# Loads ahead of masks, batch 1's attention at other slots, and a down-projection by tile in a windowed-attention and mixer kernel

## The chip, the core and the metric

The kernel runs on one NeuronCore of a Trainium2 chip. The metric is the device time of one execution in microseconds (us). PE is the TensorE matmul engine, PEld its weight load, DVE the VectorE, ACT the ScalarE, POOL the GpSimd engine, SP the queue of SyncE. SBUF is the on-chip memory, PSUM the memory that PE writes and DVE and ACT read. L247 is line 247 of the kernel.

## What is computed

Eight batches of 576 tokens, eight heads of 64. Each token attends to itself and the 63 tokens before it. The result x (576 x 512 for each batch) is mixed over tokens by two low-rank matrices U (576 x 32) and V (32 x 576) and passes a two-layer network with a skip.

```python
scores = scale * np.matmul(q, k.transpose(0, 1, 3, 2))
mask = (rel >= 0) & (rel < 64)
attn = softmax(np.where(mask, scores, -1e9))
x = heads_side_by_side(np.matmul(attn, v))
u = x + (x.transpose(0, 2, 1) @ U @ V).transpose(0, 2, 1)
out = u + np.maximum(u @ w_ch1, 0.0) @ w_ch2
```

Inputs and output are float32; the loads on POOL's queue turn them into bf16.

## The kernel before

The order of each engine's work is the order of the code; nothing reorders it. An instruction waits for semaphores of what it reads or overwrites.

**Attention of one batch** (`attention(b)`) is a set of pieces. T: for each of four head pairs j, PE transposes K (`TK`) and Q (`TQ`) to have the head dimension on the partitions; ACT copies K's transpose to `kt[j]`, DVE copies Q's to `qt[j]`. The transposes write PSUM tiles of the pool `ps_tp`, which has one buffer (batch 0 also uses `ps_mm`, with three). S: scores of a head pair in blocks of 64 queries and 128 keys (`SC`, PSUM pool `ps_big`, two buffers), the exponential on ACT, and a product with the 0/1 mask `maskA` on DVE; `SC8` does the ninth block of all pairs. PV: for a token tile t, the products with V and a column of ones, then the reciprocal of the sums and x on DVE (`rcp`, `xs`). U: x times the matrix U into 32-row strips of one PSUM tile (`pshh`, in the text also the down-projection), copied to `hh` by ACT. V: `hh` times the matrix V (`psv`, the up-projection) plus x gives u (`un`). For batches 0 and 1 (`alone`) a second matmul with the identity adds x, and the result is copied; later batches add x on DVE. UT: transposes of u to `uTc`, the input of the network.

**K and Q** of batches below NGR = 4 are loaded "grouped": 96 partitions, each with six neighbouring tokens, so that a row of one head is 6 x 64 x 4 = 1,536 bytes in DRAM. Their transposes take twelve matmuls for a head pair. From batch 4 on a row is one token of one head (256 bytes), loaded in ten DMAs a batch into `kn` and `qn`, and a head pair takes five transposes (`tpn`). `vB` holds V moved by 64 tokens; most of it is copied from `vA` on POOL (`shift_v`).

**The network** works in nine chunks of 512 tokens (`mlp(c)`): 16 groups of 4 matmuls for the first layer (`psA`, with a ReLU on ACT or DVE), then 16 groups of 4 for the second (`psU`; after every fourth group DVE adds u into `osb`, and SP stores it). A chunk's 32 groups are its slots 0 to 31. After each slot stand the attention pieces that the tables PLACE, PLACE_1 (batch 1) and PLACE_2 (batch 2) name for it; slot 32 stands behind the last group. Chunk c carries the rest of batch c + 1's attention. Batch 0's stands ahead of all chunks.

**POOL's queue** issues the loads of K, Q, V and the weights, and also builds the identity and the masks and does the V copies, all in the code's order. Eight semaphores serve its DMAs in turn, so that a DMA waits for the one eight before it. At the start it issues two of batch 0's eight K/Q pieces, builds the identity, issues two, builds the mask, and issues the last four.

Of the kernel before, what the change touches and what calls it, by code (L numbers as in the profile page):

```python
# [17 lines left out]
def kernel(  # L18
# [24 lines left out]
    NGR = 4  # L43
# [120 lines left out]
    nc.gpsimd.affine_select(  # L164
        out=maskA[:, :, 0, :],
        in_=maskA[:, :, 0, :],
        compare_op=ALU.is_ge,
        fill=0.0,
        base=0,
        pattern=[[0, 2], [1, W]],  # L170
        channel_multiplier=-1,
    )
    nc.gpsimd.affine_select(
        out=maskA[:, :, 1:, :],
        in_=maskA[:, :, 1:, :],
        compare_op=ALU.is_ge,
        fill=0.0,
        base=-1,
        pattern=[[0, 2], [0, NB - 2], [-1, W]],
        channel_multiplier=1,  # L180
    )
    nc.gpsimd.affine_select(
        out=maskA[:, :, 1:, :],
        in_=maskA[:, :, 1:, :],
        compare_op=ALU.is_ge,
        fill=0.0,
        base=W,
        pattern=[[0, 2], [0, NB - 2], [1, W]],
        channel_multiplier=-1,
    )  # L190
    for _ in kq0:
        pass
    load_v(0)
# [32 lines left out]
    def attention(b, spare=False, alone=False):  # L226
# [10 lines left out]
        def tr(src, j):  # L237
            if grouped:
                if spare and turn[0] % 4 != 0:
                    tpb = ps_mm.tile([P, 2 * CH], BF16, name="tpm", tag="mm")  # L240
                    tp = tpb[:, 0:S].rearrange("d (c p) -> d c p", c=GR)
                else:
                    tp = ps_tp.tile([P, GR, GP], BF16, name="tpg", tag="tp")
                turn[0] += 1
                for c in range(GR):
                    for g in range(2):
                        nc.tensor.transpose(  # L247
                            tp[g * D : (g + 1) * D, c, :], src[:, 2 * j + g, c, :], ident[0:GP, 0:GP]
                        )
                return tp.rearrange("d c p -> d p c")  # L250
            tp = ps_tp.tile([P, NT, P], BF16, name="tpn", tag="tp")
            for t in range(NT):
                nc.tensor.transpose(  # L253
                    tp[:, t, :],
                    src[:, t, 2 * j : 2 * j + 2, :].rearrange("p h d -> p (h d)"),
                    ident[:],
                )
            return tp.rearrange("d t p -> d (t p)")[:, 0:S]
# [9 lines left out]
        def TQ(j):  # L268
            def f():
                nc.vector.tensor_copy(out=like(qt[j][:]), in_=tr(qb, j))  # L270
            return f
# [71 lines left out]
        def U():  # L343
            ps = ps_big.tile([P, 2, CH], FP32, name="pshh", tag="big")
            for t in (0, 1, 2, 3, 4):
                g = t % 4
                nc.tensor.matmul(  # L347
                    ps[g * R : (g + 1) * R, 0, :],
                    ub[odd][:, t, :],
                    x[:, t, :, :].rearrange("p h d -> p (h d)"),  # L350
                    start=(t < 4),
                    stop=(t == 4 or t in (1, 2, 3)),
                )
            hh["sb"] = wk_pool.tile([P, CH], BF16, name="hh", tag="hh")
            nc.scalar.copy(out=hh["sb"][:], in_=ps[:, 0, :])  # L355

        def VM(ts):
            def f():
                ps = ps_big.tile([P, 2, CH], FP32, name="psv", tag="big")
                for n, t in enumerate(ts):  # L360
# [6 lines left out]
                        stop=not alone,  # L367
                    )
                    if alone:
# [7 lines left out]
                for n, t in enumerate(ts):  # L377
# [5 lines left out]
                    if alone:  # L383
                        copy = nc.scalar.copy if n else nc.vector.tensor_copy
                        copy(out=u_tiles[g][lo:hi, :], in_=ps[lo:hi, n, :])
                        continue
# [28 lines left out]
        pcs["U"] = [U]  # L415
# [7 lines left out]
    def mlp(c):  # L423
# [65 lines left out]
    PLACE_2["S"] = [3, 5, 7, 9, 10]  # L489
# [4 lines left out]
    for j in range(HP):  # L494
        a["T"][2 * j]()
        a["T"][2 * j + 1]()
        if j > 0:
            a["S"][j - 1]()
        if j == 1:
            for i in range(2):  # L500
                nc.vector.tensor_copy(out=ub[i][:], in_=uf[i][:])
            nc.vector.tensor_copy(out=vrep[:, W : W + S], in_=vf[:])
    a["S"][HP - 1]()
    a["S"][HP]()
    for _ in load_kq(2, False):
        pass
    for f in a["PV"]:
        f()
    for part in ("U", "V", "UT"):
        for f in a[part]:  # L510
            f()
    load_v(2)


    for c in range(NCH):
# [10 lines left out]
        if b < B:  # L526
            shift_v(b, nc.gpsimd.tensor_copy)
            if 3 <= b + 1 < B:
                load_v(b + 1)
            if 4 <= b + 2 < B:  # L530
# [3 lines left out]
            if b <= 2:  # L534
                place(b, ("T",), where)
            place(b, ("S", "PV"), where)
# [3 lines left out]
            if b == 1:  # L540
                slots[NSLOT - 4].append(lambda: [None for _ in load_kq(3, False)])
# [34 lines left out]
```

## Time and profile before

| what | us |
|---|---|
| three runs, median (lowest, highest) | 368.05 (364.64, 369.66) |
| the profiled execution, its own time | 367.98 |
| its span | 366.2 |
| PE busy / DVE / ACT / POOL | 341.7 / 182.5 / 123.7 / 112.1 |

The profile is of one execution. Its span is the time from the first to the last instruction. A row of the timeline gives the start, the time and the engine of an instruction or of several alike in a row, what it writes and reads, and in brackets how long the engine was idle before it and what ended that. A matmul row's time includes its way through the array, so that neighbours overlap; the distance between two starts is what a matmul costs in a stream.

### The profile page before, as it was taken

The numbers are of one execution on the slowest core, as the hardware profiler recorded it, in microseconds if no ns is written. First come the engines' busy times: TensorE is split into PE (matmuls) and PEld (weight loads), VectorE is DVE, ScalarE is ACT, GpSimd is POOL, SyncE is SP. The second block draws the span as 40 slices with busy tenths as digits, with TensorE's granted clock in tenths as the row PEclk, the third lists the DMA queues.
The fourth block names the chain that finished last, engine by engine and source line by source line (L and its number), as shares of the span: only waits on it lengthen the run. The fifth ranks groups of instructions, "written<-read, shape, count | busy, mean of one in ns | idle before, by whom it ended". The sixth has DMA issues, their size and how long they took to land.

```text
span 366.2 us, 7144 instructions
## 1 busy us (share of the span) xinstructions
PE 341.7 (93%) x3082; PEld 168.1 (46%) x3082; DVE 182.5 (50%) x319; ACT 123.7 (34%) x188; POOL 112.1 (31%) x128
## 2 busy tenths in 40 slices
PE   2779997689999999999999999999999999999995
PEld 1534444334454445544554455445544444444442
DVE  4763425935665357535753575257535753322321
ACT  2604323136513362346233522462236213301300
POOL 8891172793079004570448034000000000000000
PEclk9999999989999999999999999999999999999999
DMA  8999999795099107990869047100120011011002
GB/s 123 147 210 207 189 184 183 114 142 38 3 87 167 57 2 46 109 157 2 54 89 169 0 32 94 57 2 2 42 74 0 2 60 57 0 42 74 0 35 82
DMA packets 91135, 28.69 MB, mean 78 GB/s; under 512 B 77152, under 2 KB 85344, under 8 KB 91104
## 3 DMA queue, kind: packets, MB, share of 16 engines
q0 software_dynamic: 84512, 18.36, 58.6%
q1 hardware_dynamic: 6592, 9.88, 7.9%
q8 instruction: 24, 0.39, 0.4%
q14 instruction: 7, 0.06, 0.1%
HBM read 37.14 MB, written 9.44 MB: 127 GB/s over the span
## 4 chain that ended last, share of the span: by engine, by line
PE 86%; DVE 6%; ACT 3%; POOL 2%; DMA 1%; issue 1%; ACTq 0%; POOLq 0%
PE psA L431 35%; PE psU L453 32%; PE xr L323 3%; PE tpn L253 3%; PE psv L362 3%; PE sc L277 3%; PE tpg L247 2%; PE tpu L404 2%; DMA kg<-in_k_dram 1%; DVE pts L293 1%; PE pshh L347 1%; DVE xs_97 L333 1%; ACT pts L292 1%; PE psv L370 1%; DVE xs_98 L333 1%
## 5 line engine op out<-in xcount | busy, mean ns | idle before, releaser
L431 PE MATMUL psA<-uTc,w1b 128*128 128x512 bf16 x576 | 132.9, 380 | 1.1 <-ACT uTc L409 1.1
L431 PEld LDWEIGHTS <-w1b 128*128 128x128 bf16 x576 | 53.0, 98 | 61.2 <-issue 1.1
L462 DVE TENSOR_TENSOR osb<-psU,un 128x512 f32<-128x512 f32 x36 | 24.8, 689 | 56.5 <-PE psU L453 56.4
L293 DVE TENSOR_TENSOR pts<-pts,maskA 128x1024 bf16<-128x1024 bf16 x32 | 24.4, 765 | 33.2 <-ACT pts L292 33.2
L292 ACT ACTIVATE pts<-sc 128x1024 bf16<-128x1024 f32 x32 | 32.6, 1022 | 13.1 <-PE sc L277 13.1
L124 POOL DMA_DIRECT2D vA_100<-in_v_dram x16 | 14.1, 885 | 44.4 <-PE xr L323 37.8
L409 ACT COPY uTc<-tpu 128x512 bf16<-128x512 bf16 x27 | 15.8, 585 | 28.2 <-PE tpu L404 28.2
L124 POOL DMA_DIRECT2D vA_99<-in_v_dram x16 | 14.1, 882 | 34.9 <-PE xr L323 29.0
L323 PEld LDWEIGHTS <-pts 128*64 128x64 bf16 x576 | 14.6, 115 | 20.3 <-issue 9.4
L362 PE MATMUL psv<-hh,vrep 128*128 128x512 bf16 x40 | 15.4, 434 | 1.3 <-ACT hh L355 1.3
L404 PEld LDWEIGHTS <-un 128*128 128x128 bf16 x144 | 11.1, 102 | 7.7 <-issue 0.6
L333 DVE TENSOR_TENSOR xs_98<-xr,rcp 128x512 bf16<-128x512 f32 (+1 forms) x20 | 13.8, 692 | 0.7
L333 DVE TENSOR_TENSOR xs_97<-xr,rcp 128x512 bf16<-128x512 f32 (+1 forms) x20 | 13.8, 690 | 0.7
L247 PE MATMUL tpg<-ident,kg 96*64 96x96 bf16 x168 | 6.7, 219 | 6.4 <-DMA kg<-in_k_dram 4.6
L332 DVE RECIPROCAL rcp<-xr 128x8 f32<-128x8 f32 (+1 forms) x40 | 8.1, 204 | 8.6 <-PE xr L323 8.6
L387 DVE TENSOR_TENSOR un<-psv,xs_98 128x512 bf16<-128x512 f32 (+1 forms) x15 | 9.8, 685 | 5.2 <-PE psv L362 5.2
L247 PEld LDWEIGHTS <-kg 96*64 96x64 bf16 x192 | 6.3, 122 | 13.3 <-DMA kg<-in_k_dram 7.3
L355 ACT CAST hh<-pshh 128x512 bf16<-128x512 f32 x8 | 4.7, 589 | 22.2 <-PE pshh L347 22.2
L404 PE MATMUL tpu<-ident,un 128*128 128x128 bf16 x120 | 11.8, 222 | 0.0
L323 PE MATMUL xr<-vA_100,pts 128*64 128x65 bf16 x160 | 9.1, 197 | 2.9 <-DVE xs_98 L333 1.5
L387 DVE TENSOR_TENSOR un<-psv,xs_97 128x512 bf16<-128x512 f32 (+1 forms) x15 | 9.5, 681 | 3.4 <-PE psv L362 3.4
L115 POOL DMA_DIRECT2D kn_104<-in_k_dram x10 | 8.8, 877 | 4.9 <-PE tpn L253 4.9
(575 smaller groups left out, 628.2 us busy)
## 6 DMA issues: line engine op xcount, KB each, us to landing
out_dram<-osb SPq DMA_DIRECT2D x36, 256.0 KB, 2.1
vA_99<-in_v_dram POOLq DMA_DIRECT2D x16, 128.0 KB, 5.7
w1b<-in_moe_w_ch_dram POOLq DMA_DIRECT2D x2, 1024.0 KB, 12.7
w2b<-in_moe_w_ch_dram POOLq DMA_DIRECT2D x2, 1024.0 KB, 15.7
vA_100<-in_v_dram POOLq DMA_DIRECT2D x16, 128.0 KB, 4.7
kg<-in_k_dram POOLq DMA_DIRECT2D x3, 576.0 KB, 13.6
qg<-in_q_dram POOLq DMA_DIRECT2D x3, 576.0 KB, 14.7
kn_103<-in_k_dram POOLq DMA_DIRECT2D x8, 128.0 KB, 4.3
```

The source lines that it names most:

```text
L124: nc.gpsimd.dma_start(out=va[:, t, :, 0:D], in_=v[b, :, t * P : (t + 1) * P, :].rearrange("h p d -> p h d"),)
L247: nc.tensor.transpose(tp[g * D : (g + 1) * D, c, :], src[:, 2 * j + g, c, :], ident[0:GP, 0:GP])
L292: nc.scalar.activation(out=dst, in_=sc[:], func=ACT.Exp, scale=scale)
L293: nc.vector.tensor_tensor(out=dst, in0=dst, in1=maskA.rearrange("p g n w -> p g (n w)"), op=ALU.mult)
L323: nc.tensor.matmul(xr[r0 : r0 + W, h // 4, (h % 4) * VW : (h % 4 + 1) * VW], pts[:, h // 2, h % 2, blk, :], rhs, start=True, stop=True,)
L333: nc.vector.tensor_tensor(out=x[lo:hi, t, :, :].rearrange("p (a h) d -> p a h d", a=2), in0=xv[:, :, :, 0:D], in1=rcp[lo:hi].to_broadcast( ...
L362: nc.tensor.matmul(ps[:, n, :], vrep[:, off : off + P], hh["sb"][:], start=True, stop=not alone,)
L387: nc.vector.tensor_tensor(out=u_tiles[g][lo:hi, :], in0=ps[lo:hi, n, :], in1=x[lo:hi, t, :, :].rearrange("p h d -> p (h d)"), op=ALU.add,)
L404: nc.tensor.transpose(tp[:, dc, :], u_tiles[g][:, dc * P : (dc + 1) * P], ident[:])
L431: nc.tensor.matmul(ps[:], w1b[:, dc, i * P : (i + 1) * P], uTc[:, dc, :], start=(dc == 0), stop=(dc == NDC - 1),)
L453: nc.tensor.matmul(acc[t][:], c1[i][:, t * P : (t + 1) * P], w2b[:, i, :], start=(i == 0), stop=(i == NFC - 1),)
L462: nc.vector.tensor_tensor(out=osb[:], in0=acc[t][:], in1=u_tiles[g][:], op=ALU.add)
```

## The change

It moves and changes these things:

- The identity starts from a memset on DVE, and all eight K/Q pieces of batch 0 are issued with only the identity's select between them. The mask is built for three blocks of one head half (three selects of 64 columns on POOL); two DVE copies, after the transposes of the second head pair, spread it over the rest. V of batch 0 is issued right after the selects. The casts of U and V on DVE move from behind the second pair's transposes to behind the third's.
- NGR goes from 4 to 2, so batches 2 and 3 are loaded and transposed as batch 4 is.
- The loads of batch 2's K, Q and V move from batch 0's attention to the start of chunk 0, behind the V shift of batch 1, and batch 3's K and Q from slot 28 of chunk 0 to right behind them.
- Batch 1's Q transposes use `ps_big`. Its pieces move to earlier slots.
- The down-projection is split by token tile. In batch 0 tile t follows PV of tile t + 1; in batch 1 tiles have slots of their own. Its PSUM tile, for these two batches, is of `ps_mm`.
- In batches 0 and 1 the first tile of each up-projection group has no identity matmul, and DVE adds x.

```diff
-    NGR = 4
+    NGR = 2
...
     kq0 = load_kq(0, True)
+    nc.vector.memset(ident[:], 0.0)
     next(kq0)
     next(kq0)
-    make_identity(nc, ident[:])
-    next(kq0)
-    next(kq0)
-    nc.vector.memset(maskA[:], 1.0)
+    nc.gpsimd.affine_select(
...
+    nc.vector.memset(maskA[:, 0, 0:2, :], 1.0)
+    for _ in kq0:
+        pass
...
+    load_v(0)
...
+                elif wide:
+                    tpw = ps_big.tile([P, 2, 2 * CH], BF16, name="tpw", tag="big")
...
-                nc.vector.tensor_copy(out=like(qt[j][:]), in_=tr(qb, j))
+                nc.vector.tensor_copy(out=like(qt[j][:]), in_=tr(qb, j, alone and not spare))
...
-                        stop=not alone,
-                    )
-                    if alone:
+                        stop=not (alone and n),
+                    )
+                    if alone and n:
...
-        pcs["U"] = [U]
+        pcs["U"] = [UM((t,)) for t in range(NT)] if alone else [UM(tuple(range(NT)))]
...
     PLACE_1 = {
-        "T": [21, 22, 23, 24, 25, 26, 27, 27],
-        "S": [23, 25, 27, 28, 28],
-        "PV": [29, 30, 31, 32, 32],
-        "U": [32],
-        "V": [32, 32, 32],
+        "T": [20, 20, 21, 21, 22, 22, 23, 23],
+        "S": [21, 22, 23, 24, 24],
+        "PV": [25, 26, 27, 28, 29],
+        "U": [27, 28, 29, 30, 30],
+        "V": [31, 32, 32],
         "UT": [32, 32, 32, 32, 32],
     }
...
-    PLACE_2["S"] = [3, 5, 7, 9, 10]
+    PLACE_2["S"] = [3, 6, 9, 11, 12]
...
+        if j == 1:
+            nc.vector.tensor_copy(
+                out=maskA[:, 0, 2:, :],
+                in_=maskA[:, 0, 1:2, :].to_broadcast([P, NB - 3, W]),
+            )
+            nc.vector.tensor_copy(out=maskA[:, 1, :, :], in_=maskA[:, 0, :, :])
         if j > 0:
             a["S"][j - 1]()
-        if j == 1:
+        if j == 2:
             for i in range(2):
                 nc.vector.tensor_copy(out=ub[i][:], in_=uf[i][:])
             nc.vector.tensor_copy(out=vrep[:, W : W + S], in_=vf[:])
...
+    a["PV"][0]()
+    for t in range(NT):
+        if t + 1 < NT:
+            a["PV"][t + 1]()
+        a["U"][t]()
...
             shift_v(b, nc.gpsimd.tensor_copy)
-            if 3 <= b + 1 < B:
+            if b == 1:
+                for _ in load_kq(2, False):
+                    pass
+            if b + 1 < B:
                 load_v(b + 1)
-            if 4 <= b + 2 < B:
+            if b + 2 < B and b != 2:
                 for _ in load_kq(b + 2, False):
                     pass
...
+            if b == 2:
+                slots[8].append(lambda: [None for _ in load_kq(4, False)])
```

What stands on the queues, at three places. First POOL at the start, from the third K/Q piece's neighbourhood on, before (a row gives line, operation, what it writes and reads, and the shape):

```order
L106 DMA kg<-in_k_dram 96x2x384
L106 DMA qg<-in_q_dram 96x2x384
L164 AFFINE_SELECT maskA<-maskA 128x2x64
L173 AFFINE_SELECT maskA<-maskA 128x2x448
L182 AFFINE_SELECT maskA<-maskA 128x2x448
L106 DMA kg<-in_k_dram 96x2x384
```

and after the change:

```order
L148 AFFINE_SELECT ident<-ident 128x128
L105 DMA kg<-in_k_dram 96x2x384
L105 DMA qg<-in_q_dram 96x2x384
L105 DMA kg<-in_k_dram 96x2x384
L105 DMA qg<-in_q_dram 96x2x384
L105 DMA kg<-in_k_dram 96x2x384
L105 DMA qg<-in_q_dram 96x2x384
L162 AFFINE_SELECT maskA<-maskA 128x64 x3
```

The selects moved behind the last K/Q piece and became shorter. Second DVE in batch 0's scores, before (`qt0` to `qt3` are the head pairs' Q, the TENSOR_TENSOR rows the mask products; numbers are buffers):

```order
L270 COPY qt1_112<-tpm_223 128x576
L293 TENSOR_TENSOR pts_115<-pts_115,maskA_88 128x2x512
L501 CAST ub0_93<-uf0_91 128x160
L501 CAST ub1_94<-uf1_92 128x160
L502 CAST vrep_95<-vf_96 128x576
L270 COPY qt2_113<-tpm_273 128x576
```

and after:

```order
L263 COPY qt1_112<-tpm_223 128x576
L497 COPY maskA_88<-maskA_88 128x384
L501 COPY maskA_88<-maskA_88 128x512
L286 TENSOR_TENSOR pts_115<-pts_115,maskA_88 128x2x512
L263 COPY qt2_113<-tpm_272 128x576
L286 TENSOR_TENSOR pts_115<-pts_115,maskA_88 128x2x512
L506 CAST ub0_93<-uf0_91 128x160
L506 CAST ub1_94<-uf1_92 128x160
L507 CAST vrep_95<-vf_96 128x576
L263 COPY qt3_114<-tpm_322 128x576
```

Two mask copies stand ahead of the first product, and the casts ahead of the last Q copy. Third DVE in the second half of chunk 0, before (`osb` rows are the network's):

```order
L462 TENSOR_TENSOR osb_671<-psU_654,un_492 128x512
L270 COPY qt0_111<-tpg_701 128x576
L462 TENSOR_TENSOR osb_719<-psU_674,un_494 128x512
L293 TENSOR_TENSOR pts_115<-pts_115,maskA_88 128x2x512
L270 COPY qt1_112<-tpg_760 128x576
L293 TENSOR_TENSOR pts_115<-pts_115,maskA_88 128x2x512
L270 COPY qt2_113<-tpg_815 128x576
L462 TENSOR_TENSOR osb_833<-psU_755,un_501 128x512
L270 COPY qt3_114<-tpg_850 128x576
```

and after:

```order
L461 TENSOR_TENSOR osb_686<-psU_669,un_489 128x512
L263 COPY qt0_111<-tpw_708 128x576
L263 COPY qt1_112<-tpw_740 128x576
L286 TENSOR_TENSOR pts_115<-pts_115,maskA_88 128x2x512
L263 COPY qt2_113<-tpw_791 128x576
L286 TENSOR_TENSOR pts_115<-pts_115,maskA_88 128x2x512
L461 TENSOR_TENSOR osb_828<-psU_689,un_491 128x512
L263 COPY qt3_114<-tpw_845 128x576
```

All four Q copies now stand ahead of the third `osb`, one chunk quarter earlier.

More of the change, by code (lines that the diff above doesn't have):

```diff
@@ L7 @@
 from concourse._compat import with_exitstack
-from concourse.masks import make_identity
 ACT = mybir.ActivationFunctionType
@@ L235, in attention, with tr @@
         turn = [0]
-        def tr(src, j):
+        def tr(src, j, wide=False):
             if grouped:
@@ L341, in attention, with UM, f @@
         hh = {}
[L343 to L355, printed above, removed]
+        def UM(ts):
+            def f():
+                if ts[0] == 0:
+                    if alone:
+                        hh["ps"] = ps_mm.tile([P, CH], FP32, name="psh", tag="mm")
+                    else:
+                        hh["ps"] = ps_big.tile([P, 2, CH], FP32, name="pshh", tag="big")[:, 0, :]
+                for t in ts:
+                    g = t % 4
+                    nc.tensor.matmul(
+                        hh["ps"][g * R : (g + 1) * R, :],
+                        ub[odd][:, t, :],
+                        x[:, t, :, :].rearrange("p h d -> p (h d)"),
+                        start=(t < 4),
+                        stop=(t > 0),
+                    )
+                if ts[-1] == NT - 1:
+                    hh["sb"] = wk_pool.tile([P, CH], BF16, name="hh", tag="hh")
+                    nc.scalar.copy(out=hh["sb"][:], in_=hh["ps"])
+            return f
         def VM(ts):
```

61 lines of the change are left out of this document (21 added, 40 removed).

## The prediction

> **What bounds the kernel now.** I read the page's head and its chain first, then a table of windows by stage, then the timeline of the two stages that are not steady. The page says that TensorE carries the time: its span, and the chain by engine.
>
> ```profile
> span 366.2 us, 7144 instructions
> PE 86%; DVE 6%; ACT 3%; POOL 2%; DMA 1%; issue 1%; ACTq 0%; POOLq 0%
> L292 ACT ACTIVATE pts<-sc 128x1024 bf16<-128x1024 f32 x32 | 32.6, 1022 | 13.1 <-PE sc L277 13.1
> ```
>
> 86% is an average. The windows below are cut where a stage starts on PE: batch 0's attention up to its hh, its up-projection and transposes, first-layer matmuls of chunk 0 (psA), the rest of chunk 0 (psU with batch 1's attention between) and, inside it, its end, then chunks 1 and 2. The second figure is the length, the third PE's busy time; the granted clock stands third from the end.
>
> ```profile
> 0.00:24.85 24.85, 12.59 (x245) 9.12 (x246) 15.28 (x37) 8.79 (x11) 22.43 (x36) 1.00 1.27 155
> 24.85:31.32 6.47, 5.80 (x26) 2.92 (x26) 2.82 (x5) 2.27 (x4) 2.98 (x4) 1.00 1.19 206
> 31.32:45.13 13.81, 13.81 (x64) 6.26 (x64) 4.84 (x7) 4.78 (x8) 2.24 (x3) 1.00 1.45 197
> 45.13:80.62 35.49, 28.21 (x341) 13.91 (x339) 19.28 (x30) 9.77 (x14) 23.77 (x24) 0.95 1.67 156
> 69.37:80.62 11.25, 7.65 (x85) 3.78 (x84) 7.00 (x16) 2.83 (x5) 10.31 (x13) 0.85 1.80 129
> 80.62:122.63 42.01, 41.72 (x491) 20.42 (x491) 23.56 (x40) 16.73 (x26) 21.29 (x22) 1.00 0.96 77
> 122.63:160.05 37.42, 37.42 (x344) 18.66 (x343) 20.25 (x36) 15.05 (x23) 13.49 (x16) 1.00 0.70 65
> ```
>
> From 80.62 us on PE has no idle time to give (41.72 of 42.01, 37.42 of 37.42). What waits is ahead of that: 12.3 us of the first 24.85, and 7.3 us of the 35.49 in which batch 1's attention stands between the psU groups; the end of that stage also runs at a granted clock of 0.85. A psU or psA matmul takes 13.81/64 = 0.216 us. The change touches exactly these places, so I cost it stage by stage.
>
> **Stage A: start to the first psA (31.32 us before).** Timeline rows of the start, all engines:
>
> ```profile
> 4.57 0.31 POOL L164 TENSOR_SCALAR_AFFINE_SELECT maskA<-maskA 128x128 bf16<-128x128 bf16 x1
> 6.89 0.64 POOL L106 DMA_DIRECT2D kg<-in_k_dram  x1
> 11.39 0.69 DVE L293 TENSOR_TENSOR pts<-pts,maskA 128x1024 bf16<-128x1024 bf16 x1 [0.90 <-ACT pts L292]
> 12.00 0.23 DVE L501 CAST ub_93<-uf_91 128x160 bf16<-128x160 f32 x1
> 13.12 0.74 DVE L270 COPY qt_113<-tpm 128x576 bf16<-128x576 bf16 x1
> 13.36 0.69 PE L247 MATMUL tpm<-ident,kg 96*64 96x96 bf16 x12 [0.88 <-DMA kg<-in_k_dram]
> 13.78 0.67 DVE L293 TENSOR_TENSOR pts<-pts,maskA 128x1024 bf16<-128x1024 bf16 x1
> 14.84 0.76 DVE L270 COPY qt_114<-tpm 128x576 bf16<-128x576 bf16 x1 [0.39 <-PE tpm L247]
> 20.24 0.23 PE L323 MATMUL xr<-vB_101,pts 128*64 128x65 bf16 x1 [0.92 <-DVE rcp L332]
> 24.21 0.58 ACT L355 CAST hh<-pshh 128x512 bf16<-128x512 f32 x1 [6.41 <-PE pshh L347]
> 24.85 0.59 PE L362 MATMUL psv<-hh,vrep 128*128 128x512 bf16 x1 [0.67 <-ACT hh L355]
> 25.23 0.63 PE L370 MATMUL psv<-xs_97,ident 128*128 128x512 bf16 x1
> ```
>
> - Loads before masks. On POOL's queue the last four K/Q issues move from behind the selects, 6.89, to about 4.57: up to 2.3 us. PE did wait for them (13.36, on kg). But DVE's order changes with them: the three casts of U and V (12.00 to the copy at 13.12, so 1.1 us) now stand after the second mask product, right ahead of the qt_114 copy. That product can start at best some 0.6 us sooner, since its exponential follows the first one (1.02 us) on ACT: it ends near 13.8, the casts near 14.9, and qt_114 is copied at 14.9, against 14.84 now. What is late next after the load is the cast. Bounds 0 and 2.3; I take 0.2, nearest to the DVE row.
> - Mask products from copies: two bf16 copies of 384 and 512 columns on DVE, new, no such row. A 1024-column product takes 0.69, so some 0.6 for both; without cover they cost that. They stand before the product at 11.39, ahead of which DVE idled 0.90: 0. The small ident and mask memsets lie in DVE's idle start, the three shorter selects on POOL now stand ahead of the V loads, not the K/Q loads.
> - Down-projection by tile. The last of five matmuls waited for the last xs before and does so still: no gain. Three of them now stand ahead of the next PV on PE. A matmul of 512 columns takes 0.4 here (24.85 to 25.23). PE was waiting for DVE (0.92 at 20.24), but for the same event that now releases the extra matmul, so DVE's next reciprocal comes later. Cost 0 to 3 x 0.4 = 1.3; I take 0.5, since only the first is not behind an xs product.
> - Up-projection: three of ten matmuls (the identity ones of tiles 0, 2, 4) go, 3 x 0.43 = 1.3; DVE adds where it copied, both 128x512 from PSUM. I take 1.2, bounds 0 and 1.3.
>
> A: 0.2 + 0 - 0.5 + 1.2 = +0.9 (bounds -1.9 and +3.6). First psA at 30.4.
>
> **Stage B: the rest of chunk 0 (35.49 us before).** Its rows:
>
> ```profile
> 50.40 0.45 PE L247 MATMUL tpg<-ident,kg 96*64 96x96 bf16 x12
> 50.78 0.39 PE L453 MATMUL psU<-w2b,c_8_603 128*128 128x512 bf16 x1
> 53.47 0.41 PE L277 MATMUL sc<-qt_111,kt_107 64*128 64x64 bf16 x16
> 53.81 0.39 PE L453 MATMUL psU<-w2b,c_0_547 128*128 128x512 bf16 x1
> 57.26 0.45 PE L247 MATMUL tpg<-ident,kg 96*64 96x96 bf16 x12 [1.06 <-DVE qt_112 L270]
> 66.96 0.25 PE L323 MATMUL xr<-vA_100,pts 128*64 128x65 bf16 x2 [1.36 <-DVE pts L293]
> 70.35 0.68 DVE L462 TENSOR_TENSOR osb<-psU,un 128x512 f32<-128x512 f32 x1
> 73.60 0.38 PE L347 MATMUL pshh<-xs_98,ub_94 128*32 128x512 bf16 x1 [0.44 <-DVE xs_98 L333]
> 74.65 0.59 PE L362 MATMUL psv<-hh,vrep 128*128 128x512 bf16 x1 [0.67 <-ACT hh L355]
> 75.03 0.63 PE L370 MATMUL psv<-xs_98,ident 128*128 128x512 bf16 x1
> 75.46 0.63 PE L362 MATMUL psv<-hh,vrep 128*128 128x512 bf16 x1
> 80.62 1.02 PE L431 MATMUL psA<-uTc,w1b 128*128 128x512 bf16 x4 [0.38 <-ACT uTc L409]
> ```
>
> The waits come from the one transpose buffer (57.26: K's transpose waits for Q's copy), from the mask products (66.96), and from the end, where after the last psU four PV-to-xs steps, hh, ten matmuls at 0.43 (75.03 to 75.46) and five transposes stand with nothing between. In the changed order the Q transposes use other buffers, PV and the down-projection stand among the psU groups, and after the last psU only four of seven psv and five transposes are left.
>
> PE's work there: 64 x 0.216 = 13.8; eight transposes of a head pair at 0.38 (50.40 to 50.78), 3.0; scores 4 x 0.34 and the short one, 1.5; PV 1.7 (five groups of scores' size at most); five single 512-column matmuls 1.1, seven psv 1.5, both at 0.216 as PE no longer stands still ahead of them; five uT transposes 1.1; some nine changes between psU and others at 0.09, 0.8. Sum 24.5. Waits that stay, by walking the new order with DVE's 0.69 to 0.76 and ACT's 1.02: the fourth scores for qt_114, 0.6; the first PV for the fourth mask product, 0.8; and at the end DVE's osb, three un and two uTc copies against 2.6 of PE work, 1.8. Stage: 24.5 + 3.2 = 27.7, rounded to 27.5. Gain 8.0. Bounds: no wait, 35.5 - 24.5 = 11.0; the 7.3 of idle time kept, 35.5 - 31.8 = 3.7. I take 8.0 since every wait in the sum is from a row's duration. Chunk 1 then starts at 30.4 + 13.8 + 27.5 = 71.7.
>
> **Stage C: chunk 1 (42.01 before).** Batches 2 and 3 are now transposed 128 wide: five matmuls in place of twelve, as batch 4's K is in chunk 2:
>
> ```profile
> 140.86 0.45 PE L253 MATMUL tpn<-ident,kn_103 128*128 128x128 bf16 x5
> 141.15 0.38 PE L453 MATMUL psU<-w2b,c_4_1823 128*128 128x512 bf16 x1
> ```
>
> 0.29 against 0.38: 16 x 0.09 = 1.4, I take 1.5. Below: 0, if a wait fills it; above: chunk 2's 37.42 plus eight more at 0.29 is 39.7, a gain of 2.3. Later chunks and the tail are unchanged.
>
> **Sum.** 0.9 + 8.0 + 1.5 = 10.4, a span of 355.8. The profiled execution took 367.98, 1.78 more than its span and 0.07 less than the median of 368.05, so I predict 357.6 us.
>
> **Rivals.** (1) PE meets the first psA at half speed. Batch 0's psv ran 0.43 apart and in the change fewer of them, with gaps, stand ahead of psA. In the end of chunk 0 the 0.43 lasted 3.3 us at a granted 0.85. If as long a stretch falls on psA, it costs half of it, 1.7: 359.3. For it: less PE work before; against: the transposes still stand there. *The Trainium skill, "TensorE: Matmul & The Clock Gate", Part 1, says that PE starts at half clock and is released after about 3.4 us of sustained work in a free-running window; the trace's 3.3 us agrees, and by that rule the loss here hangs on where the window falls.*
>
> (2) POOL's V shift (3.4 us) falls on batch 1's first mask products. Rows of it, and of the K/Q loads behind it:
>
> ```profile
> 52.57 1.90 POOL L136 COPY vB_102<-vA_100 64x2048 bf16<-64x2048 bf16 x1
> 55.24 1.29 DVE L293 TENSOR_TENSOR pts<-pts,maskA 128x1024 bf16<-128x1024 bf16 x1 [1.28 <-ACT pts L292]
> 74.22 0.90 POOL L115 DMA_DIRECT2D kn_103<-in_k_dram  x1
> DMA to landing us min/median/max: 3.3/4.7/6.2
> ```
>
> A product beside such a copy took 1.29 against 0.69; two or three on the path are 1.6: 359.2.
>
> (3) The packing meets the waits it had: B gives its lower bound 3.7, and the time is 361.9. For it: scores, exponentials and products are the same chain on ACT and DVE; against: ACT is busy 9.8 and DVE 19.3 of 35.5.
>
> (4) The side on which it is slower: batch 2's K and Q come late. They now stand on POOL behind the shift of batch 1's V and go out as ten issues, not two. If the shift ends no sooner than before (52.57 + 3.4 = 56.0), ten issues at 0.87 end at 64.7 and land at the median 4.7 later, 69.4; chunk 1's first transpose wants them at 71.7. Each us later costs one; past a landing at 82.1 the kernel is slower than before, past 89.5 by 2%. For it: the margin is 2.3 us; against: the slowest of 40 such landings took 6.2. At 8 us over the margin it is 365.6. *The Trainium skill, "DMA: Bandwidth & Descriptors", Specifications, says that transfers under 512 B miss the line rate, and these rows shrink from 1,536 to 256 B; by that rule the landing goes past 71.7, the trace's 6.2 us does not show it.*
>
> **Chances.** My forecast 0.60, with a range of its own of 355 to 359.5; (1) 0.13; (2) 0.10; (3) 0.12; (4) 0.05, of which 0.02 past 2%. The range of 354.0 to 361.5 leaves out most of (3), (4) and a little of the forecast, 0.2. Two per cent, about what a measurement can tell from no change here, is 360.7: faster holds nearly all of the forecast, (1) and (2), 0.79; same 0.18; slower 0.03.
>
> **What would show it.** First psA at 29.5 to 31.3, with qt_114 copied at 14.5 to 15.1 right behind the casts; no wait of K's transpose for a Q copy; psv of batch 1 at 0.22; chunk 1's psA near 71.7, its length near 40.5 with tpn in place of tpg, and kn landed before. Wrong if chunk 1's first transpose waits for a DMA, if PE's idle time between 44 and 72 stays above 6 us, or if the first psA are 0.43 apart.

## Result and profile after

The changed kernel takes 356.78 us (median of four runs, 356.05 to 357.29), the kernel before in the same comparison 368.18 (364.64 to 369.66): a ratio of 0.970, 95% interval 0.964 to 0.977. The forecast was 357.6 (354.0 to 361.5). A later comparison on another occasion, six runs of the changed kernel against eleven of the kernel before, gave 357.80 (357.56 to 357.92), ratio 0.975 (0.971 to 0.980).

The page's head and its chain by engine:

```profile
span 354.3 us, 6888 instructions
PE 331.5 (94%) x2914; PEld 166.7 (47%) x2964; DVE 177.3 (50%) x322; ACT 123.6 (35%) x188; POOL 124.3 (35%) x143
PE 77%; DMA 12%; POOL 8%; issue 2%; ACT 1%; DVE 0%; POOLq 0%
```

PE's count is 2914 matmuls against 2964 weight loads, so some 50 matmul records are missing here, and its 94% is a little too low. The 12% of DMA and 8% of POOL in the chain are of this execution alone: in the last profile of the same kernel, taken beside the filled kernel below, they are 2% and 1%, with the same lengths of chunk 0's rest and of chunk 1, and the list of PE's waits in chunk 1 is empty. So they do not show that loads bound the kernel.

The windows, cut at the same events as before (hh, first psA, first psU, the end of chunk 0, chunks 1 and 2):

```profile
0.00:24.68 24.68, 13.29 (x245) 9.34 (x246) 14.83 (x40) 8.21 (x11) 22.15 (x36) 1.00 1.29 164
24.68:29.50 4.82, 2.67 (x22) 1.65 (x23) 2.69 (x5) 2.83 (x5) 2.01 (x3) 1.00 1.19 205
29.50:43.31 13.81, 13.75 (x63) 6.26 (x64) 4.84 (x7) 4.78 (x8) 0.69 (x1) 1.00 1.37 201
43.31:70.64 27.33, 24.88 (x332) 13.12 (x336) 16.53 (x30) 9.69 (x14) 21.05 (x23) 1.00 1.69 124
64.00:70.64 6.64, 5.32 (x37) 2.76 (x38) 4.41 (x9) 2.84 (x5) 6.64 (x9) 1.00 2.60 167
70.64:110.81 40.17, 39.52 (x372) 20.82 (x378) 21.61 (x40) 16.60 (x26) 36.22 (x40) 1.00 1.79 124
110.81:148.21 37.40, 37.09 (x338) 18.66 (x342) 20.26 (x36) 15.07 (x23) 15.85 (x18) 1.00 0.83 78
```

| stage | before | forecast | after | gain |
|---|---|---|---|---|
| start to hh | 24.21 | | 24.68 | -0.47 |
| hh to first psA | 7.11 | | 4.82 | 2.29 |
| A: start to first psA | 31.32 | 30.4 | 29.50 | 1.82 |
| chunk 0's psA | 13.81 | 13.8 | 13.81 | 0 |
| B: rest of chunk 0 | 35.49 | 27.5 | 27.33 | 8.16 |
| C: chunk 1 | 42.01 | 40.5 | 40.17 | 1.84 |

That is 11.82 of the 11.9 us by which the span fell. (hh's row starts at 24.68; the first psA at 29.50.) The end of chunk 0 now runs at a granted 1.00, not 0.85. The waits of PE between 43.31 and 70.64 (engine, line, waited for: total, times, longest):

```profile
PE psv L362 <- ACT un L384: 0.8, 1, 0.8
PE psU L452 <- issue: 0.6, 4, 0.2
PE xr L316 <- DVE pts L286: 0.4, 1, 0.4
PE tpu L403 <- DVE uTc L408: 0.2, 1, 0.2
PE sc L270 <- DVE qt_114 L263: 0.2, 1, 0.2
```

No K transpose waits for a Q copy any more. The start, by its timeline rows (start, time, engine, what; in brackets the idle time ahead):

```profile
7.88 0.69 PE L240 MATMUL tpm<-ident,kg 96*64 96x96 bf16 x12 [1.66 <-DMA kg<-in_k_dram]
10.45 0.25 DVE L497 COPY maskA<-maskA 128x384 bf16<-128x384 bf16 x1
10.73 0.29 DVE L501 COPY maskA<-maskA 128x512 bf16<-128x512 bf16 x1
11.37 0.69 DVE L286 TENSOR_TENSOR pts<-pts,maskA 128x1024 bf16<-128x1024 bf16 x1 [0.35 <-ACT pts L285]
13.90 0.66 DVE L506 CAST ub_93<-uf_91 128x160 bf16<-128x160 f32 x1
14.99 0.75 DVE L263 COPY qt_114<-tpm 128x576 bf16<-128x576 bf16 x1
15.79 0.61 PE L270 MATMUL sc<-qt_114,kt_110 64*128 64x64 bf16 x16 [1.90 <-DVE qt_114 L263]
24.27 0.38 PE L345 MATMUL psh<-xs_97,ub_93 128*32 128x512 bf16 x1 [0.48 <-DVE xs_97 L326]
25.74 0.38 PE L370 MATMUL psv<-xs_97,ident 128*128 128x512 bf16 x1
25.96 0.59 PE L362 MATMUL psv<-hh,vrep 128*128 128x512 bf16 x2
```

The mask copies cost 0.54 and end with 0.35 of idle time still behind them: hidden in this execution. The casts stand right ahead of the qt_114 copy, and PE waits 1.90 for it. The one surprise is in the last two rows: one psv stands 0.22 behind the one before, where before the change all ten stood 0.43 apart. And batch 2's loads, the danger of rival 4: the shift, the last of the ten issues, and the first transpose that needs them:

```profile
49.54 1.90 POOL L135 COPY vB_102<-vA_100 64x2048 bf16<-64x2048 bf16 x1 [15.36 <-DMA vA_100<-in_v_dram]
61.06 0.76 POOL L114 DMA_DIRECT2D qn_105<-in_q_dram  x1
qn_105<-in_q_dram POOLq DMA_DIRECT2D x12, 128.0 KB, 4.8
71.50 0.44 PE L246 MATMUL tpn<-ident,kn_103 128*128 128x128 bf16 x5
```

The last issue stands at 61.06. With the median of 4.8 us to landing that is 66, and 5 us are to spare.

### The profile page after: what moved, and what is told of

Its sections match the earlier page's. It is cut to its first block, busy times and chain, and to the rows that moved or that the text cites. A ratio compares the mean times of both kernels' runs of the same rounds, so it can differ in the third digit from the quotient of the medians.

```text
span 354.3 us, 6888 instructions
## 1 busy us (share of the span) xinstructions
PE 331.5 (94%) x2914; PEld 166.7 (47%) x2964; DVE 177.3 (50%) x322; ACT 123.6 (35%) x188; POOL 124.3 (35%) x143
## 3 DMA queue, kind: packets, MB, share of 16 engines
q0 software_dynamic: 100128, 18.36, 66.7%
## 4 chain that ended last, share of the span: by engine, by line
PE 77%; DMA 12%; POOL 8%; issue 2%; ACT 1%; DVE 0%; POOLq 0%
PE psU L452 31%; PE psA L430 31%; DMA vA_100<-in_v_dram 6%; PE tpn L246 4%; DMA w1b<-in_moe_w_ch_dram 4%; PE xr L316 3%; PE sc L270 2%; PE psv L362 2%; POOL vA_99 L123 2%; PE tpu L403 2%; DMA kn_104<-in_k_dram 2%; POOL qn_105 L114 1%; POOL kn_103 L114 1%; PE pshh L345 1%; POOL qg L105 1%
## 5 line engine op out<-in xcount | busy, mean ns | idle before, releaser
L430 PE MATMUL psA<-uTc,w1b 128*128 128x512 bf16 x555 | 131.3, 380 | 1.8 <-ACT uTc L408 0.7
L286 DVE TENSOR_TENSOR pts<-pts,maskA 128x1024 bf16<-128x1024 bf16 x32 | 23.2, 725 | 33.2 <-ACT pts L285 33.2
L114 POOL DMA_DIRECT2D kn_104<-in_k_dram x15 | 13.7, 911 | 7.9 <-PE tpn L246 7.9
L386 DVE TENSOR_TENSOR un<-psv,xs_98 128x512 bf16<-128x512 f32 (+1 forms) x18 | 11.9, 688 | 5.7 <-PE psv L362 5.6
L114 POOL DMA_DIRECT2D kn_103<-in_k_dram x15 | 13.3, 884 | 4.0 <-PE tpn L246 4.0
L386 DVE TENSOR_TENSOR un<-psv,xs_97 128x512 bf16<-128x512 f32 (+1 forms) x18 | 11.5, 684 | 5.7 <-PE psv L362 3.8
L362 PE MATMUL psv<-hh,vrep 128*128 128x512 bf16 x38 | 12.1, 379 | 2.3 <-ACT un L384 1.6
L114 POOL DMA_DIRECT2D qn_106<-in_q_dram x15 | 13.8, 917 | 1.4 <-PE tpn L246 1.4
L326 DVE TENSOR_TENSOR xs_98<-xr,rcp 128x512 bf16<-128x512 f32 (+1 forms) x20 | 13.8, 692 | 0.7
L326 DVE TENSOR_TENSOR xs_97<-xr,rcp 128x512 bf16<-128x512 f32 (+1 forms) x20 | 13.8, 690 | 0.7
L135 POOL COPY vB_102<-vA_100 64x2048 bf16<-64x2048 bf16 x4 | 7.6, 1896 | 18.5 <-DMA vA_100<-in_v_dram 18.4
L114 POOL DMA_DIRECT2D qn_105<-in_q_dram x15 | 13.4, 890 | 1.0 <-PE tpn L246 1.0
```

Source lines behind the costliest of these rows:

```text
L114: nc.gpsimd.dma_start(out=dst[0:rows, t, :, :], in_=src[b, :, t * P : t * P + rows, :].rearrange("h p d -> p h d"),)
L286: nc.vector.tensor_tensor(out=dst, in0=dst, in1=maskA.rearrange("p g n w -> p g (n w)"), op=ALU.mult)
L326: nc.vector.tensor_tensor(out=x[lo:hi, t, :, :].rearrange("p (a h) d -> p a h d", a=2), in0=xv[:, :, :, 0:D], in1=rcp[lo:hi].to_broadcast( ...
L362: nc.tensor.matmul(ps[:, n, :], vrep[:, off : off + P], hh["sb"][:], start=True, stop=not (alone and n),)
L386: nc.vector.tensor_tensor(out=u_tiles[g][lo:hi, :], in0=ps[lo:hi, n, :], in1=x[lo:hi, t, :, :].rearrange("p h d -> p (h d)"), op=ALU.add,)
L430: nc.tensor.matmul(ps[:], w1b[:, dc, i * P : (i + 1) * P], uTc[:, dc, :], start=(dc == 0), stop=(dc == NDC - 1),)
```

## Experiments

Line numbers are those of each kernel. Unless said otherwise, each experiment is one execution, with its profile. The time from start to first psA varies between executions of one and the same code, so its parts are also read from the second Q copy (qt_112: 9.73 before, 9.77 after).

**The changed kernel again**, unaltered.

> The changed kernel once more, unaltered, as a measure of how far stage times repeat. Expected: first psA of chunk 0 at 29.5 us, chunk 0's second layer stage (first psU to chunk 1's first psA) 27.3, chunk 1 40.2, each within 0.3; psv of batch 0 0.22 apart after the first.

It took 357.98 us: A 31.16, B 27.58, C 40.16. The second Q copy came at 11.08, 1.3 us later than in the first profile, and the first psA 1.7 later; hh to psA 4.83, psv again 0.22 apart. So B and C repeat to 0.3 us, A only to some 2.

**Batch 1's Q transposes in the one buffer** (packed slots kept):

```diff
-                nc.vector.tensor_copy(out=like(qt[j][:]), in_=tr(qb, j, alone and not spare))
+                nc.vector.tensor_copy(out=like(qt[j][:]), in_=tr(qb, j))
```

> Batch 1's Q transposes go back to the single transpose buffer, at the new slots. Theory (the second set of buffers is what lets the packed slots run): each Q transpose waits for ACT's copy of K's, about 0.7 us four times, and the stage from chunk 0's first psU to chunk 1's first psA grows from 27.3 to 29.5 to 30.5 us. Rival (the slots alone do it, the waits lie beside ACT and DVE work that bounds anyway): 27.3 to 27.8.

361.59 us, B 30.98 (+3.65, a little beyond the range expected), C 40.16. PE's largest wait in B:

```profile
PE tpg L240 <- ACT kt L258: 3.1, 4, 0.8
```

The wait is back, four times 0.8, the other way round than before (Q's transposes wait for K's copies). Without the second set of buffers the packed slots lose 3.65 us of what B gained; 4.51 of it stays.

**Batch 1's pieces at their old slots** (buffers and down-projection by tile kept):

```diff
-        "T": [20, 20, 21, 21, 22, 22, 23, 23],
-        "S": [21, 22, 23, 24, 24],
-        "PV": [25, 26, 27, 28, 29],
-        "U": [27, 28, 29, 30, 30],
-        "V": [31, 32, 32],
+        "T": [21, 22, 23, 24, 25, 26, 27, 27],
+        "S": [23, 25, 27, 28, 28],
+        "PV": [29, 30, 31, 32, 32],
+        "U": [32, 32, 32, 32, 32],
+        "V": [32, 32, 32],
```

> Batch 1's pieces at the slots of before (its five down-projection pieces in slot 32), all else as changed. Theory (the slots carry most of the stage's gain of 8.2 us, since PV, down- and up-projection then stand bare behind the last psU): the stage is 32.5 to 34.5 us, with psv slow (0.43 apart) again. Rival (buffers and fewer matmuls carry it): 28 to 30.

361.45 us, B 30.48 (+3.15), C 40.16. That lies between the two ranges: I had the slots down for more. The windows of B and of its last 7 us:

```profile
45.58:76.06 30.48, 27.39 (x338) 13.34 (x337) 16.43 (x30) 9.68 (x14) 24.13 (x27) 0.94 1.87 122
69.00:76.06 7.06, 5.51 (x30) 2.44 (x30) 3.70 (x8) 2.83 (x5) 5.26 (x7) 0.76 2.92 153
```

PE's waits there sum to 2.9 us, against 2.2 in the changed kernel. More than half of the loss is the clock: 7.06 us at a granted 0.76 give away 0.24 x 7.06 = 1.7. With nothing between the attention's last pieces the clock was lost after PE had idled, as before the change (11.25 at 0.85, also 1.7); with psU groups between them it was not.

**x added by a matmul in all tiles again** (ten psv, five of them with the identity, as before):

```diff
-                        stop=not (alone and n),
+                        stop=not alone,
...
-                    if alone and n:
+                    if alone:
```

(and DVE copies instead of adding).

> The identity matmuls of the first tile of each up-projection group come back (ten psv matmuls in batches 0 and 1), all else as changed. Theory (three matmuls at 0.22 to 0.43): hh of batch 0 to the first psA grows by 0.4 to 1.3 against the same clock, chunk 0's stage from 27.3 to 27.6 to 28.0. Rival (DVE's un copies bind, not PE): both unchanged within 0.2.

358.95 us, B 27.69 (+0.36), hh to psA of batch 0 6.68. All of its psv stood 0.43 apart, so it is to be held against the executions with that pace below (5.8 to 6.0): three matmuls are worth 0.7 to 0.9 there and 0.36 in B, at full pace (3 x 0.22 = 0.66 if nothing covered them).

**Batches 2 and 3 transposed in groups** again (this also changes their K and Q loads back):

```diff
-    NGR = 2
+    NGR = 4
```

> Batches 2 and 3 are loaded and transposed grouped again (twelve matmuls for a head pair), all else as changed. Theory (chunk 1's gain of 1.84 us is the 16 transposes at 0.29 in place of 0.38): chunk 1 grows from 40.2 to 41.6 to 42.0, chunk 0 unchanged. Rival (it comes from the changed score slots of batch 2): 40.2 to 40.5.

361.6 us, B 27.32, C 43.05 (+2.88): more than I expected, and more than the 42.01 of the kernel before. In its chunk 1 a wait stands that neither kernel has:

```profile
PE psA L430 <- DVE c L439: 0.7, 1, 0.7
```

The change also moved batch 2's scores to later slots, and 42.01 was measured with the old ones; that the twelve-matmul pieces fit the new slots worse is the likely reason, not tried alone. The narrow transposes, with their loads, are thus worth 2.88 us at the new slots, while C as a whole gained 1.84.

**The down-projection behind all PV**, for batch 0:

```diff
-    a["PV"][0]()
-    for t in range(NT):
-        if t + 1 < NT:
-            a["PV"][t + 1]()
-        a["U"][t]()
+    for f in a["PV"]:
+        f()
+    for f in a["U"]:
+        f()
```

> Batch 0's five down-projection matmuls stand behind all of PV again; all else as in the changed kernel. Theory 1 (the matmuls between the PV groups keep PE's clock up, so that psv runs 0.22 apart): psv goes back to 0.43 apart; hh is some 0.5 us sooner (24.2), the first psA some 0.5 to 1.0 later (30.0 to 30.5). Rival (psv is fast whatever stands before it, the three removed matmuls did the rest): psv stays 0.22 apart, hh 0.5 sooner, first psA 0.5 sooner (29.0).

357.3 us, first psA 30.77. From the second Q copy to hh 14.37, against 14.91 and 15.25 in the two executions of the changed kernel above: by tile costs 0.5 to 0.9 us here, since U's matmuls stand ahead of the next PV and DVE waits for that. psv stood 0.43 apart, and hh to psA took 6.42. That is what theory 1 says, but it does not tell it from its rival: with the code of the changed kernel psv ran 0.43 apart in four of six executions too (below).

**U one PV later** (two PV ahead of the first U, then alternating):

```diff
     a["PV"][0]()
+    a["PV"][1]()
     for t in range(NT):
-        if t + 1 < NT:
-            a["PV"][t + 1]()
+        if t + 2 < NT:
+            a["PV"][t + 2]()
         a["U"][t]()
```

> In batch 0 each down-projection matmul stands behind the PV group two tiles on, not one. Theory (the three matmuls ahead of the next PV cost DVE the three idle times of 0.42, 0.18 and 0.18 us): those idle times go, hh comes 0.5 to 0.8 sooner (23.9 to 24.2) and the first psA at 28.7 to 29.0 with psv still 0.22 apart. Rival (PV waits for DVE in any case): no change, 29.5.

358.18 us. DVE's first idle time of 0.42 ahead of a reciprocal is gone, the two of 0.18 stay; qt_112 to hh 14.80, 0.1 to 0.5 sooner, less than the theory had. psv 0.43 apart, hh to psA 5.93, first psA 31.67: no gain.

**The casts of U and V on ACT**, behind the last exponential:

```diff
-        if j == 2:
-            for i in range(2):
-                nc.vector.tensor_copy(out=ub[i][:], in_=uf[i][:])
-            nc.vector.tensor_copy(out=vrep[:, W : W + S], in_=vf[:])
...
     a["S"][HP]()
+    for i in range(2):
+        nc.scalar.copy(out=ub[i][:], in_=uf[i][:])
+    nc.scalar.copy(out=vrep[:, W : W + S], in_=vf[:])
```

> The three casts of U and V are taken off DVE and done on ACT behind batch 0's last exponential. Theory (the casts ahead of the qt_114 copy eat what the earlier loads bring): qt_114 is copied at about 13.4 in place of 14.99, the fourth mask product ends some 1.0 to 1.5 us sooner and the first psA comes at 28.0 to 28.8. Rival (the V shift on POOL, which ends at 19.9, binds PV next): first psA at 29.2 to 29.5.

357.91 us. qt_114 comes 4.75 behind the second Q copy, hh 14.62. In the six executions with the changed kernel's start (below) these are 4.97 to 5.84 and 14.91 to 15.33: the casts cost the start 0.3 to 0.7 us up to hh, in the direction that the prediction gave them, and less than the 1.0 to 1.5 expected of the fourth mask product. The second Q copy itself came late (10.80), psv were 0.43 apart again, hh to psA 5.97, and the first psA came at 31.39, not at 28.0 to 28.8; so the kernel is no faster in this execution.

**The masks first**, as before the change (full mask by POOL's selects ahead of the last four K/Q loads):

```diff
+    next(kq0)
+    next(kq0)
+    nc.vector.memset(maskA[:], 1.0)
+    nc.gpsimd.affine_select(
...
-        if j == 1:
-            nc.vector.tensor_copy(
-                out=maskA[:, 0, 2:, :],
-                in_=maskA[:, 0, 1:2, :].to_broadcast([P, NB - 3, W]),
-            )
-            nc.vector.tensor_copy(out=maskA[:, 1, :, :], in_=maskA[:, 0, :, :])
```

> The changed kernel with the masks as before: full mask built on POOL by selects ahead of the last four K/Q loads, and no mask copies on DVE. Theory (the casts of U and V, not the loads, set when qt_114 is copied, as the prediction had it): the third pair's transposes wait for their load again (0.5 to 1 us), the casts and the qt_114 copy come 0 to 0.7 us later against the second Q copy (after: 5.2, again: 5.8), hh 14.9 to 15.9 us after the second Q copy; the loads ahead of the masks are worth 0 to 0.7 us. Rival (the loads are what the start was waiting for): qt_114 7 us or more and hh 16.5 us or more after the second Q copy, a loss of 1.5 to 2.3 us. Chunk 0's rest 27.3 and chunk 1 40.2 in both.

358.68 us, first psA 32.15. Against the second Q copy hh comes at 16.69, which is the rival's range. But that yardstick moved: the copy came at 9.03, sooner than in any of the twelve executions with the loads ahead (9.77 to 11.08), though the loads of the second pair go out at the same time, 3.09 and 3.73, in both. Its rows for the second K, the second Q and the third K:

```profile
7.35 0.69 PE L258 MATMUL tpm<-ident,kg 96*64 96x96 bf16 x12 [1.24 <-DMA kg<-in_k_dram]
8.29 0.69 PE L258 MATMUL tpm<-ident,qg 96*64 96x96 bf16 x12 [0.25 <-DMA qg<-in_q_dram]
10.85 0.69 PE L258 MATMUL tpg<-ident,kg 96*64 96x96 bf16 x12 [1.32 <-DMA kg<-in_k_dram]
```

With the masks first the second K is there at 7.35 (7.42 before the change), with the loads ahead at 7.88 (the profile after) to 9.16 (the kernel again), in all twelve. So the four loads that go out earlier come with a later second pair; that they share the DMA engines with it is the likely reason, not a shown one. In absolute time the first psA is 0.1 to 1.0 later than in the four executions whose code up to there is the changed kernel's and whose psv are 0.43 apart (31.14 to 32.06, below). But about 0.5 us of that lies behind hh, where the code is the same (6.43 against 5.80 to 5.97). hh itself comes at 25.72, inside the 24.68 to 26.33 of the six executions with the changed kernel's start. So no gain of this part is shown, and neither is a loss.

**Six more matmuls in PE's gaps.** With psv at one pace in some executions and another in the rest, the clock had to be tried. The results are not used:

```diff
+        def warm(n):
+            if "ps" not in hh:
+                hh["ps"] = ps_mm.tile([P, CH], FP32, name="psh", tag="mm")
+            for _ in range(n):
+                nc.tensor.matmul(hh["ps"][:], ident[:], kt[0][:, 0:CH], start=True, stop=True)
...
+    a["warm"](3)
     a["S"][HP - 1]()
     a["S"][HP]()
+    a["warm"](2)
     a["PV"][0]()
...
+        if t == 0:
+            a["warm"](1)
         a["U"][t]()
```

> The changed kernel with six more matmuls on PE in batch 0's attention, each 128x512 of a ready kt against the identity matrix, written into the psh accumulator ahead of its first real matmul, which overwrites them: three where PE idled 1.90 us for qt_114, two ahead of the first PV (0.90), one ahead of the first down-projection (0.59). Theory A (how busy PE was just before decides its pace): the idle ahead of psv is mostly gone, so batch 0's psv stand 0.22 apart, hh to the first psA takes 4.7 to 4.9 us, and the PV groups and psh before are faster too (a psh 0.38, not 0.6); hh is no later than 15.2 us after the second Q copy (after: 14.9, again: 15.3). Rival (the pace hangs on where the execution happens to lie, six matmuls do not change it): psv 0.43 apart, hh to psA 5.9 to 6.0, hh 0 to 0.6 us later for the matmuls. Chunk 0's rest stays 27.3 and chunk 1 40.2 in both.

357.84 us, psv 0.43 apart, hh to psA 5.66: neither theory as it stood. Rows of three down-projections (the first fast), and windows on both sides of 21.7:

```profile
20.89 0.38 PE L353 MATMUL psh<-xs,ub 128*32 128x512 bf16 x1 [1.07 <-DVE xs L326]
21.73 0.59 PE L353 MATMUL psh<-xs,ub 128*32 128x512 bf16 x1
25.03 0.59 PE L353 MATMUL psh<-xs,ub 128*32 128x512 bf16 x1 [0.47 <-DVE xs L326]
18.30:21.70 3.40, 1.67 (x50) 1.29 (x51) 3.32 (x7) 0.46 (x1) 3.28 (x5) 1.00 1.12 211
21.70:28.50 6.80, 5.40 (x33) 2.17 (x34) 3.36 (x7) 0.59 (x2) 4.83 (x7) 0.50 1.16 210
```

In this execution the full clock came some 6 us sooner than in the profile after (there the first fast row is the psh at 24.27). But then PE, at full speed, idled half of the next 3.4 us (1.67 busy), and the clock was taken back for 6.8 us, over psv.

**The gaps filled throughout**, and the casts on ACT as above (`fill` is `warm` into a tile of its own, `psw`):

```diff
...
+    a["warm"](2)
     a["S"][HP - 1]()
     a["S"][HP]()
...
+    a["warm"](2)
     a["PV"][0]()
     for t in range(NT):
         if t + 1 < NT:
             a["PV"][t + 1]()
+        a["fill"](1)
         a["U"][t]()
+    a["fill"](2)
```

> The changed kernel with the three casts of U and V on ACT behind the last exponential, and eleven more matmuls of 128x512 on PE in batch 0's attention, whose results are not used: two behind the third scores, two ahead of the first PV, one ahead of each of the five down-projections, two ahead of psv. Theory (PE's recent work decides: in the run with six such matmuls the records show the clock released near 18.1 us and taken back at 21.7, after a stretch in which PE idled half the time): with the later gaps filled too, the clock is not taken back, psv stand 0.22 apart, hh to the first psA takes 4.9 or less, hh comes 0 to 0.5 us sooner against the second Q copy than in the changed kernel (14.9 to 15.3 there); median 354.5 to 356.5. Rival (the phase of the execution decides, the fillers do not hold it): psv 0.43 apart in the look, hh to psA 5.9 to 6.4, hh later by up to 1.5 us; median 357 to 359, no better than the changed kernel.

356.14 us (six runs, 355.49 to 357.39), ratio to before 0.972 (0.967 to 0.976).

**The changed kernel timed beside it**, unaltered:

> The changed kernel once more, timed in the same call as the filled one: 356 to 358.2 in every run (356.05 to 357.29 and 357.98 so far). Its psv 0.43 or 0.22 apart, by the execution; hh to psA 5.9 or 4.8 with it.

357.80 (357.56 to 357.92). The medians differ by 1.66 us and the two sets of runs do not overlap; the intervals of the two ratios do, because the kernel before scatters by 6 us. Rows of the filled kernel, then of the changed one, from U's last matmul to psv:

```profile
23.33 0.38 PE L361 MATMUL psh<-xs,ub 128*32 128x512 bf16 x1
24.38 0.59 PE L378 MATMUL psv<-hh,vrep 128*128 128x512 bf16 x2
24.81 0.38 PE L386 MATMUL psv<-xs,ident 128*128 128x512 bf16 x1
```

```profile
24.72 0.59 PE L345 MATMUL psh<-xs,ub 128*32 128x512 bf16 x1 [0.47 <-DVE xs L326]
25.98 1.01 PE L362 MATMUL psv<-hh,vrep 128*128 128x512 bf16 x2 [0.67 <-ACT hh L354]
26.78 0.63 PE L370 MATMUL psv<-xs,ident 128*128 128x512 bf16 x1
```

All five psh of the filled kernel take 0.38, and its psv follow each other at 0.22 where no un copy holds them. hh stands 13.92 behind the second Q copy (15.11 in the changed kernel beside it; 14.62 with the casts alone on ACT), hh to psA is 4.82 (5.80); B gave 0.40 back (27.72 against 27.32). It is the version that I would keep, by a gain of about 0.5% that rests on one occasion: the changed kernel's first four runs (356.05 to 357.29) lie inside the filled kernel's range. What the matmuls do without the casts was not tried.

## Why the prediction was right

**B (8.0 forecast, 8.16 measured): right, and by its parts.** The work was put at 24.5 and the waits at 3.2 (a sum of 27.7, which was then rounded to 27.5); measured are 2.2 of waits and so 25.1 of work and changes. Of the single waits, 0.6 for qt_114 is 0.2, 0.8 for the first PV is 0.4, 1.8 at the end is 1.0; another 0.6 is issue. Undone one at a time, the buffers carry 3.65, the slots 3.15 (1.7 of it the clock), the three identity matmuls 0.36: 7.16 of 8.16. The last 1.0 was not tried: the down-projection by tile inside B, or parts that work together.

**C (1.5 forecast, 1.84): right in kind.** The transposes are 0.28 apart (71.50 to the psA at 71.78), 0.10 less than before, and 16 of these are 1.6.

**A (0.9 forecast, 1.82 in the profile): not confirmed.** Up to hh the prediction had 0.2 - 0.5 = -0.3 and -0.47 came; qt_114 was forecast at 14.9 and copied at 14.99. The term that fell short is the up-projection: 1.2 forecast, 2.29 measured. It counted three matmuls fewer at the pace that psv had before, 0.43. In this execution the other psv ran at 0.22 as well. In the changed kernel's execution beside the filled one they ran at 0.43, and there hh to psA took 5.80, a gain of 1.31: the size forecast, but not by the three matmuls alone. With all ten psv back it took 6.68, so they are worth 0.7 to 0.9. The other 0.43 between 6.68 and the 7.11 before lies behind the last psv, where the transposes ran faster (the four of `tpu` in 0.23, not 0.43).

A as a whole repeats worst. In the six executions with the changed kernel's start the first psA came at 29.50, 31.14, 31.16, 31.40, 31.77 and 32.06, against 31.32 in the one profile before: between 1.8 sooner and 0.7 later. The profile with the result is the earliest of them. In the execution beside the filled kernel A gained 0.18, not 0.9, because hh came at 25.34, 1.13 later than before, where 0.3 later was forecast. That its span of 356.0 is so near the forecast 355.8 is luck: B and C made 0.5 more than forecast, and A 0.7 less. What carries the prediction is B and C, 9.5 forecast and 10.0 measured in both profiles.

What sets the pace of psv is not the order alone. Six executions have the same code up to the first psA: the three of the changed kernel, and those with one buffer, old slots and grouped batches. Two of them had psv at 0.22 and four at 0.43, and that is worth 1.0 to 1.2 us. Six more matmuls went with a full clock that came early and was lost again, eleven with one that stayed. These are one profile each, so they fit PE's recent work as a cause beside the moment of the execution, and do not prove it. *The Trainium skill, "TensorE: Matmul & The Clock Gate", Part 1, puts the gate on a free-running window of about 3.4 us; the 6.8 us at half clock in the run with six are two such windows, and the two paces of one code fit a window whose phase differs from one execution to the next.* That the phase is the cause in these six executions is argued: their windows show a granted clock of 1.00 there throughout.

**The loads ahead of the masks: 0.2 was taken, and nothing was shown.** That the casts come next is borne out in part by the run with the casts on ACT (0.3 to 0.7 us up to hh). What the prediction did not see is the second pair's later landing.

**The rivals.** (1) PE at half clock on the first psA: did not come; chunk 0's psA took 13.81 us in every profile, 64 times 0.216. Its clock did cost about 1 us in four of the six executions, but earlier, on psv.

(2) The shift on the mask products: in the profile after it ran from 49.54 to 53.49, and the four products of batch 1, from 51.47 to 56.92, all took 0.69. In other executions it did come. First the kernel again, then the filled kernel, with the second copy of the shift and products beside it:

```profile
52.74 1.47 POOL L136 COPY vB<-vA 64x1536 bf16<-64x1536 bf16 x1
53.12 1.63 DVE L286 TENSOR_TENSOR pts<-pts,maskA 128x1024 bf16<-128x1024 bf16 x1 [0.64 <-ACT pts L285]
```

```profile
51.20 1.81 POOL L136 COPY vB<-vA 64x1536 bf16<-64x1536 bf16 x1
50.53 1.15 DVE L286 TENSOR_TENSOR pts<-pts,maskA 128x1024 bf16<-128x1024 bf16 x1 [0.64 <-ACT pts L285]
52.47 1.08 DVE L286 TENSOR_TENSOR pts<-pts,maskA 128x1024 bf16<-128x1024 bf16 x1
PE sc L270 <- DVE qt L263: 0.6, 1, 0.6
```

B was 0.25 and 0.40 longer there, not the 1.6 of the rival. In the filled kernel PE's wait for a Q copy was 0.6 in place of 0.2. The shift starts when V of batch 1 has landed (POOL waits 15.0 us for it there), so an earlier start of the chunks can move the products onto it. In the run with the casts on ACT a product took 1.28 and B stayed 27.32, so not every such product is on the path.

(3) Packing meets the same waits: with one buffer it does. That kernel's 361.59 is close to the 361.9 of this rival, but its B still gained 4.5, not 3.7.

(4) Late K and Q of batch 2: by the median landing they were there 5 us ahead. The landing times do not compare row sizes, since the 4.7 us that the prediction took is of loads with 256-byte rows too. What the smaller rows cost stands in the pages' lines of POOL's DMA queue (packets, MB, and the packets' time as a share of 16 engines' span), before, after, and with batches 2 and 3 grouped again:

```profile
q0 software_dynamic: 84512, 18.36, 58.6%
q0 software_dynamic: 100128, 18.36, 66.7%
q0 software_dynamic: 84512, 18.36, 60.1%
```

The same 18.36 MB took 215 us of all 16 engines before, 236 after and 216 grouped (share times span): about 20 us more for the rows of 256 B, which PE's work covered. *The Trainium skill, "DMA: Bandwidth & Descriptors", Specifications, puts transfers under 512 B below line rate; these lines agree in direction.*

## What to carry to other kernels

Packing attention between matmul groups pays in full only together with enough transpose buffers: each without the other leaves over 3 of 8 us here. Where a stage alternates with short stalls, price its matmuls at both clocks, and count a half-clock stretch that a new order removes as part of the gain. At the start of a kernel, loads issued earlier can come with a later landing of those already under way, so read the landing of the ones ahead too. Where the start of one code varies by over 2 us between executions, a gain of 1 us there needs several profiles.

## What was not expected of the hardware

- The same code ran its first 512-column matmuls 0.43 or 0.22 us apart from one execution to the next, at up to 1.2 us for the kernel, while the windows of these executions show a granted clock of 1.00. The distance between starts tells more there than the clock column.
- A kernel with matmuls whose results are thrown away was the faster one: eleven of them on PE in gaps, together with the casts moved, went with 1.66 us less on one occasion. With six the full clock came and went again: PE was busy 1.67 of the 3.40 us at full clock.
- Loads issued at the same time were there 0.5 to 1.8 us later (the second K at 7.88 to 9.16 in twelve executions, 7.35 in the one without) when four more loads followed directly behind them.
- The 256-byte rows took about 20 us more of all 16 DMA engines for the same bytes, and that did not show in the time, since PE waited for none of them.
